# A conditioned transformer block on one core: the head's fills and loads in another order, the key path first, the queries all ended in block 0, first scores among the last maxima, two places of maxima ahead of the loop instead of three

## The chip, the cores and the metric

The kernel runs on one core of a Trainium2 chip. The metric is the device time of one execution in microseconds (us), as the median of several. A core has TensorE (PE; its weight loads are listed as PEld), VectorE (DVE), ScalarE (ACT) and GpSimd (POOL), and queues through which SyncE (SP) and ScalarE start transfers (DMA) between memory and the on-chip buffers. Each engine works through its own instructions strictly in their order, and waits at an instruction until the semaphores that it names have been raised. TensorE writes into eight banks of accumulators, from which VectorE and ScalarE read; a bank is free again when it has been read.

## What is computed

```python
mod = (_silu(c) @ w_mod).reshape(c.shape[0], 6, 1, -1)
sa, ca, ga, sb, cb, gb = (mod[:, 0], mod[:, 1], mod[:, 2], mod[:, 3], mod[:, 4], mod[:, 5])
h = _layernorm(x, axis=-1) * (1 + ca) + sa
x = x + ga * _A_ref(h, A_wq, A_wk, A_wv, A_wo)
h = _layernorm(x, axis=-1) * (1 + cb) + sb
x = x + gb * _B_ref(h, B_w1, B_w2)
```

x has 2048 rows of 512. `_A_ref` is attention with 32 query heads of 16 over one shared key head and one shared value head, softmax over all 2048 keys, then the output projection. `_B_ref` is a dense layer to 1792, relu, and a dense layer back to 512. All is float32.

## The kernel before

**Units and rounds.** The queries are cut into 8 blocks of 256 rows and 4 groups of 8 heads: 32 units. The main loop (L949) has 256 rounds, eight to a unit, two key tiles to a round. In a round stand 8 scores (`scores`, L802: a product into a `ps_exp` bank, exp on ScalarE into a `pe` tile), 8 products with the values (`values`, L936, into `ps_pv`) of scores made before, 8 maxima (`max_of`, L465: a product into a `ps_max`, `ps_more` or `ps_fill` bank, reduced by VectorE, L476) of the unit that comes next, and one portion of dense work (L171): query projections in block 0, and from block 1 on the output projection and the dense layers of the block before. Two strings, `PARTS` and `SHORT` (L43, without a portion), set the order of these within the two halves of a round. A "place" of maxima is eight of them, both halves of the heads over four key blocks of 512 columns; a unit has eight places.

**The maxima's way back.** A score is exp(q k - max), with the maximum put into the product itself: two rows of the query tile `qp` hold the negated maximum, as a high and a low part. When a unit's last maximum has been reduced (L478), VectorE transposes them (`sq<-negm`, L439), ScalarE and GpSimd split them into `ms`, and SP stores them to memory (`mdr<-ms`, L446, four transfers of 16 partitions each) and loads them back in another layout (`qp<-mdr`, L452, two transfers). Stores are issued in the next round's first half; the load stands at that round's end (L963). The unit's first score stands in the second half of the last round of the unit before it.

**The head.** Ahead of the loop stand the modulation vectors, the row norms of x, its transposition to `hT`, keys and values (`kv`, L334: four products over the depth, then evictions, then transposes of the values: five steps for each of four blocks of 512 rows), the first `HEAD_Q` = 5 of 16 query units, and 64 + `LEAD` = 88 maxima: all 64 of unit 0 and three places of unit 1. The queries go to memory (`qdr<-qq`, L370, three transfers each) and come back as `qp` tiles (`load_q`, L417). Loads of x, of the weights and of the modulation matrix `wmod` are issued by SP in program order; eight transfers are in flight at a time. The order of the head's steps is the string `FIRST` (L36), read one letter at a time (L888): `A`, `B` the two halves of the first query unit; `q` two products of a query unit (four letters to a unit); `k` a step of `kv`; `t` four transposes and their eviction; `x`, `y` row statistics on VectorE, `s` on ScalarE; `c`, `e`/`E`, `r`, `f`, `g` the scale of rows and its application; `o` half of a modulation row; `w` a product that only keeps TensorE busy; `m` one maximum; `L`, `l` loads of `qp` for units 0 and 1, and at `L` also of the four later modulation matrices. After the last letter four first scores of the loop are made (L926).

The start, ahead of the string: 32 products of the identity (`warm(32)`, L861), the condition `c` loaded as a column (L78), its silu, two modulation rows (L192) turned into columns, the first block's rows normalized on ScalarE and GpSimd (L307) and transposed with the modulation applied in the eviction (`tr1`, L318). GpSimd copies the keys' and values' weights to their layout (L137) and then fills `kp` and `vt` (L138, L139).

The query units 5 to 13 are the dense portions of block 0 (27 rounds of 32); units 14 and 15 stand in block 1, in its first three rounds and among the seven rounds in which it waits for the second row norm (L573 to L576).

## Time and profile before

| | |
|---|---|
| median of 3 runs | 1631.83 us (1631.66 to 1633.18) |
| the profiled execution | 1633.18 us |
| its span, first to last instruction | 1631.2 us |
| first value products of the loop | 99.9 us into the span |
| from 467 to 1560 us: TensorE, VectorE, ScalarE busy | 1092.5, 926.8, 868.7 of 1093 us |
| last stretch, 1560 to 1631.2: TensorE, VectorE busy | 65.0, 19.9 of 71.2 us |
| granted TensorE clock, mean over the span | 0.996 |

Times in the trace are counted from the span's start; the two microseconds between span and time lie outside it. Matmuls are pipelined and their ends are modelled, so TensorE reads as busy also where it is held for a bank; what holds it is seen in the idle time of the weight loads and in the chain of waits, which follows the work that ended last back to what released it. Each float32 product of the dense steps appears as two records.

### The profile page before, as it was taken

To read this page: it belongs to the slowest core of one execution; us is meant where nothing else is said; L and a number is where in the kernel's file an instruction comes from. 1 tells how busy PE (TensorE), PEld (TensorE's weight loads), DVE (VectorE), ACT (ScalarE), POOL (GpSimd) and SP (SyncE) were. 2 spreads that over 40 slices of the span, in tenths; PEclk is the share of its full clock that TensorE was granted. 3 is DMA by queue.
4 is the path that set the end of the run, shared out by engine and by line. 5 is a ranking of instruction groups with operands and counts; after the bars stand their busy time and mean duration, and the time that the engine had idled before them with its cause. 6 is when DMAs were issued, how large, how long until landed. Compare 5 with 4: busy or idle time off the path is not lost.

```text
span 1631.2 us, 33611 instructions
## 1 busy us (share of the span) xinstructions
PE 1612.9 (99%) x12948; PEld 909.7 (56%) x12948; DVE 1348.6 (83%) x2341; ACT 1212.6 (74%) x2372; POOL 386.5 (24%) x588
## 2 busy tenths in 40 slices
PE   8999999999999999999999999999999999999999
PEld 6545553546654565546654565546654565546668
DVE  5888889898889888998889888898889888997031
ACT  4557778778877887778877887778877887778831
POOL 3313466241113111141113111141113111141110
PEclk9999999999999999999999999999999999999999
DMA  8225633214211331213211331213211231113331
GB/s 280 87 73 170 210 95 106 80 44 125 82 30 46 91 103 33 62 42 114 81 30 48 89 102 34 61 43 113 81 30 49 88 99 37 61 43 104 123 114 57
DMA packets 96718, 137.16 MB, mean 84 GB/s; under 512 B 24564, under 2 KB 60084, under 8 KB 96560
## 3 DMA queue, kind: packets, MB, share of 16 engines
q1 hardware_dynamic: 94848, 134.89, 27.4%
q8 instruction: 103, 1.69, 0.4%
q14 instruction: 55, 0.45, 0.1%
q10 hardware_dynamic: 1712, 0.13, 0.1%
HBM read 104.00 MB, written 28.82 MB: 81 GB/s over the span
## 4 chain that ended last, share of the span: by engine, by line
PE 92%; DVE 3%; ACT 3%; DMA 2%; issue 0%; SPq 0%; POOL 0%; POOLq 0%; ACTq 0%; DVEq 0%
PE ps_pv L943 31%; PE ps_exp L806 21%; PE ps_fill L171 19%; PE ps_max L474 17%; DVE pm L476 2%; ACT pe L808 2%; PE ps_exp L154 1%; PE ps_max L154 1%; PE ps_exp L339 1%; PE ps_fill L154 1%; DMA xb<-in_A_x_dram 1%; DMA wq<-in_A_wq_dram 1%; ACT pvs L818 0%; PE ps_exp L325 0%; DMA qp<-qdr 0%
## 5 line engine op out<-in xcount | busy, mean ns | idle before, releaser
L476 DVE TENSOR_REDUCE pm<-ps_max 128x1 f32<-128x512 f32 x2006 | 1245.7, 682 | 157.6 <-PE ps_max L474 114.7
L808 ACT ACTIVATE pe<-ps_exp 128x512 f32<-128x512 f32 x2048 | 1079.5, 605 | 301.1 <-PE ps_exp L806 143.2
L474 PE MATMUL ps_max<-kp,qp 48*128 48x512 f32 x2006 | 829.6, 425 | 3.1 <-DMA qp<-qdr 2.6
L806 PE MATMUL ps_exp<-qp,kp 50*128 50x512 f32 x2048 | 764.6, 416 | 5.4 <-ACT pe L808 4.4
L943 PE MATMUL ps_pv<-pe,vt 128*32 128x512 f32 x4096 | 546.8, 605 | 0.0
L806 PEld LDWEIGHTS ps_exp<-qp,kp 50*128 50x128 f32 x2048 | 360.0, 186 | 277.9 <-ACT pe L808 187.0
L474 PEld LDWEIGHTS ps_max<-kp,qp 48*128 48x128 f32 x2006 | 366.4, 185 | 248.1 <-DVE pm L476 214.4
L171 PE MATMUL ps_fill<-w2r,r 64*128 64x512 f32 x1044 | 285.7, 404 | 0.0
L171 PE MATMUL ps_fill<-hh,w1s 64*128 64x256 f32 x1568 | 227.8, 285 | 0.0
L171 PEld LDWEIGHTS ps_fill<-hh,w1s 64*128 64x128 f32 x1568 | 204.3, 185 | 6.9 <-PEq L164 6.7
L171 PEld LDWEIGHTS ps_fill<-w2r,r 64*128 64x128 f32 x1044 | 181.9, 184 | 11.2 <-PEq L164 2.5
L943 PEld LDWEIGHTS ps_pv<-pe,vt 128*32 128x32 f32 x4096 | 81.0, 108 | 125.9 <-issue 106.3
L253 POOL TENSOR_TENSOR r<-stg,r 128x512 fp32r<-128x512 f32 x49 | 62.8, 1282 | 321.3 <-ACT r L252 314.4
L171 PE MATMUL ps_fill<-hl,w1s 64*128 64x256 f32 x784 | 126.8, 281 | 0.0
L171 PEld LDWEIGHTS ps_fill<-hl,w1s 64*128 64x128 f32 x784 | 104.7, 185 | 0.0
L171 PE MATMUL ps_fill<-hT,wq 64*128 64x256 f32 x352 | 100.8, 404 | 0.0
L985 POOL TENSOR_TENSOR on<-num,den 128x256 f32<-128x256 f32 x31 | 22.8, 735 | 220.6 <-DMA den<-recs 165.7
L171 PEld LDWEIGHTS ps_fill<-hT,wq 64*128 64x128 f32 x352 | 60.4, 189 | 3.1 <-DVE pm L476 0.4
L822 POOL COPY num<-pvs 128x256 f32<-128x256 f32 x32 | 12.7, 396 | 177.7 <-ACT pvs L818 177.7
L264 ACT ACTIVATE stg<-ps_fill 128x512 f32<-128x512 f32 x64 | 39.4, 616 | 4.9 <-PE ps_fill L154 4.9
L277 POOL TENSOR_TENSOR x<-stg,x 128x512 f32<-128x512 f32 x14 | 18.1, 1291 | 97.8 <-ACT stg L276 97.8
L253 POOL TENSOR_TENSOR ms<-sq,ms 128x32 fp32r<-128x32 f32 x32 | 8.2, 255 | 131.2 <-ACT ms L252 131.2
(158 smaller groups left out, 965.2 us busy)
## 6 DMA issues: line engine op xcount, KB each, us to landing
w1s<-w1dr SPq DMA_DIRECT2D x104, 512.0 KB
qp<-qdr SPq DMA_DIRECT2D x64, 192.0 KB
qdr<-qq SPq DMA_DIRECT2D x45, 256.0 KB
raw<-in_B_w_dram SPq DMA_DIRECT2D x28, 256.0 KB
w1dr<-w1s SPq DMA_DIRECT2D x14, 512.0 KB
wmod<-in_w_mod_dram SPq DMA_DIRECT2D x6, 1024.0 KB
x<-in_A_x_dram SPq DMA_DIRECT2D x8, 512.0 KB
out_dram<-ot SPq DMA_DIRECT2D x16, 256.0 KB
```

The lines of the kernel that those rows point to most:

```text
L154: nc.tensor.matmul(pt, w, a, start=start, stop=stop)
L171: ins = nc.tensor.matmul(pt, w[r], a[r], start=start and h == 1, stop=stop and h == 0)
L253: (eng or nc.gpsimd).tensor_tensor(lo, src, hi.bitcast(F32), op=OP.subtract)
L264: nc.scalar.activation(stg, pt, func, **kw)
L277: nc.gpsimd.tensor_tensor(dst, stg, other, op=OP.add)
L339: nc.tensor.matmul(pt, wkv[:, k * P:(k + 1) * P], hT[b][:, k], start=k == 0, stop=k == DC - 1)
L474: nc.tensor.matmul(pt, qps[u][i][r, j * P:(j + 1) * P], kp[r, kb * 512:(kb + 1) * 512], start=True, stop=True)
L476: nc.vector.tensor_reduce(pms[u][:, (hf * 2 + i) * 4 + j, kb:kb + 1], pt, axis=AX.X, op=OP.max)
L806: nc.tensor.matmul(pt, kp[r, kt * P:(kt + 1) * P], qps[u][ct // 2][r], start=True, stop=True)
L808: nc.scalar.activation(pe, pt, AF.Exp)
L943: nc.tensor.matmul(pvt[at:at + 32], vt[:, kt], pes.pop((s, i)), start=(kt == 0), stop=(kt == KT - 1))
L985: due[1]()
```

## The change

The start: `c` is loaded as four rows and transposed by TensorE (a `ps_max` bank), with the 32 warm-ups spread over four places. `wk` and `wv` are loaded by SP, behind the first query weight, and copied by GpSimd after the first rows' normalization; the fills of `kp`, `vt` and `firsts` go first. x of the fourth block and two query weights are loaded only at letter `L`, behind the queries' way back. The first block's transposes are issued two blocks of depth ahead of the second modulation column (`tr_first`), the last of the four in the `ps_fill` bank.

The string: `L` stands behind the first half of the first query unit; the first block's keys come ahead of its second half; 80 maxima, 20 query steps (six units in the head) and eight letters `d`, each one first score of the loop, among the last maxima. Round 0 has no first-half scores left.

The loop: query units 6 to 15 are all portions of block 0, and block 1's places for them are empty. The negated maxima are stored in two transfers of 128 partitions instead of four of 16, and loaded in the second half of the same round.

```diff
-LEAD = 24
-HEAD_Q = 5
-FIRST = ("AkxqxsycyqkyBkkytqELqttmmmkmmsqkrktsmmmmkkmsmommmmttqftm"
-         "mmmogtkmmmkkmmmmkktmmlmmtqmmqtmmmmkkktmmmmkkmmmmqwmmmqmk"
-         "mmmommmqmmmqmmmommmqmmqmmommmommmqmmmommqmmmommmmmmm")
+LEAD = 16
+HEAD_Q = 6
+FIRST = ("AxkkLkxxxkcwqyqkyyywBEmmmmqttqtktkmmsrmmkkmsmmmqttmmmmqs"
+         "sqtmmmmkkkfmmmmqktmmmmqgkqmmmmttqqtmmmmkkkmmmmtkmmkmmmom"
+         "mmqommmmqkmmommmqmmlmqmmmommqommmmqqqmmomddmmdmmdodmmmdd"
+         "mdo")
...
-    ccol = cst.tile([P, DC], F32, name="ccol")
-    nc.scalar.dma_start(ccol, c[0].rearrange("(k p) -> p k", p=P), allow_slow_non_contiguous=True)
+    crow = cst.tile([DC, P], F32, name="crow")
+    nc.scalar.dma_start(crow, c[0].rearrange("(k p) -> k p", p=P))
...
-    wkv0 = sb.tile([P, DC, 2, DH], F32, name="wkv0", tag="tmp", bufs=2)
-    nc.scalar.dma_start(wkv0[:, :, 0], chunks(wk))
-    nc.scalar.dma_start(wkv0[:, :, 1], chunks(wv))
...
     load_wq(0)
-    for b in range(1, NL):
-        load_x(b)
-        load_wq(b)
+    wkv0 = sb.tile([P, DC, 2, DH], F32, name="wkv0", tag="stg", bufs=3)
+    nc.sync.dma_start(wkv0[:, :, 0], chunks(wk))
+    nc.sync.dma_start(wkv0[:, :, 1], chunks(wv))
+    load_x(1)
+    load_wq(1)
+    load_x(2)
...
-    for j in range(8):
-        nc.gpsimd.tensor_copy(wkvr[:, :, j], wkv0[:, :, 1 if j % 4 == 3 else 0])
-    nc.gpsimd.memset(kp.bitcast(F32), 1.0)
-    nc.gpsimd.memset(vt, 1.0)
...
+    warm(4)
+    ccol = ps_max()[:, 0:DC]
+    nc.tensor.transpose(ccol, crow, idn[0:DC, 0:DC])
+    warm(22)
...
+    def tr_first():
+
+        h = hT[0] = sb.tile([P, DC, LB], F32, name="hT", tag="big", bufs=4)
+        pts = [turn_rows(0, k) for k in range(2)]
+        yield
+        for k in range(DC):
+            if k == 0:
+                pts += [turn_rows(0, 2), turn_rows(0, 3, ps_fill)]
+            if k % 2:
+                nc.vector.tensor_scalar(h[:, k], pts[k], cols[:, 1, k:k + 1], cols[:, 0, k:k + 1],
+                                        op0=OP.mult, op1=OP.add)
...
-            for q in range(4):
-                nc.sync.dma_start(mdr[:, :, q].rearrange("p a n -> a p n"),
-                                  ms[q * 32:q * 32 + 16].bitcast(F32))
+            for e in range(2):
+                nc.sync.dma_start(mdr[e].rearrange("a q n -> q a n"), ms[:, e].bitcast(F32))
...
-            qqs = [sb.tile([P, 2, LB], F32R, name="qq", tag="w1s", bufs=3) for _ in range(2)]
-            rest, fill = [others_of(14 + n, qqs[n]) for n in range(2)]
-            fill = itertools.chain([[]] * 3, fill, [[]])
+            rest, fill = iter([[]] * 3), [[]] * 7
...
-        for n in range(HEAD_Q, 14):
+        for n in range(HEAD_Q, 16):
...
     run(sums_of(0))
     row1 = mod_row(1, ps_max())
     ln1_rows(0, *ln1_ends(mvs[0], True))
+    warm(4)
+    for j in range(8):
+        nc.gpsimd.tensor_copy(wkvr[:, :, j], wkv0[:, :, 1 if j % 4 == 3 else 0])
+    mod_col(row1, 1, True, ps_max())
+    warm(2)
     row0 = mod_row(0, ps_max())
-    mod_col(row1, 1, True, ps_max())
+    first_rows = tr_first()
+    next(first_rows)
+    mod_col(row0, 0, False, ps_max())
+    run(first_rows)
...
+    early = [(s, ct) for cts in ((1, 3), (0, 2)) for s in range(2) for ct in cts]
...
             load_q(0)
+            load_x(3)
+            for n in (2, 3):
+                load_wq(n)
             for i in (2, 5, 3, 4):
                 load_mod(i)
...
+        elif what == "d":
+            scores(*early.pop(0))
...
-    for s, ct in ((0, 1), (0, 3), (1, 1), (1, 3)):
-        scores(s, ct)
...
-            c=[partial(scores, *n) for n in ((s, 0), (s, 2), (s + 1, 0), (s + 1, 2))],
+            c=[partial(scores, *n) for n in ((s, 0), (s, 2), (s + 1, 0), (s + 1, 2)) if c],
...
-            ends.append((c, load))
+            half_later.append(load)
```

How the rows move is shown at three places. First SP's queue in the head, from the loads of x to the first queries' way back (`xb` are blocks of x, `wq` query weights, `qdr` the queries in memory, `qp` the query tiles, `wmod` modulation); before:

```order
L97 DMA xb<-in_A_x_dram 128x512 x4
L111 DMA wq_82<-in_A_wq_dram 128x4x128
L99 DMA xb<-in_A_x_dram 128x4x512
L111 DMA wq_83<-in_A_wq_dram 128x4x128
L99 DMA xb<-in_A_x_dram 128x4x512
L111 DMA wq_83<-in_A_wq_dram 128x4x128
L370 DMA qdr_0_123<-qq 8x16x256 x6
L423 DMA qp<-qdr_0_123 48x4x256 x2
L90 DMA wmod<-in_w_mod_dram 128x4x512 x4
```

and with the change:

```order
L113 DMA wkv_82<-in_A_wk_dram 128x4x16
L114 DMA wkv_82<-in_A_wv_dram 128x4x16
L98 DMA xb<-in_A_x_dram 128x512 x4
L106 DMA wq_70<-in_A_wq_dram 128x4x128
L100 DMA xb<-in_A_x_dram 128x4x512
L388 DMA qdr_0_119<-qq 8x16x256 x3
L441 DMA qp<-qdr_0_119 48x4x256 x2
L100 DMA xb<-in_A_x_dram 128x4x512
L106 DMA wq_71<-in_A_wq_dram 128x4x128 x2
L91 DMA wmod<-in_w_mod_dram 128x4x512 x4
```

The first read of `qp` stands behind three stores instead of six, and the fourth block of x and two weights have moved behind it.

Second, TensorE where the head passes into round 0 (`ps_max`, `ps_more`: maxima; `ps_exp<-qp,kp`: scores; `ps_fill<-hT`: query projections, the first product with the values follows); before:

```order
L474 MATMUL ps_max<-kp,qp 128x512 x3
L474 MATMUL ps_more<-kp,qp 128x512
L806 MATMUL ps_exp<-qp,kp 128x512 x5
L474 MATMUL ps_max<-kp,qp 128x512
L806 MATMUL ps_exp<-qp,kp 128x512
L474 MATMUL ps_max<-kp,qp 128x512
L171 MATMUL ps_fill<-hT,wq_82 128x256
```

and with the change:

```order
L823 MATMUL ps_exp<-qp,kp 128x512
L195 MATMUL ps_exp<-wmod,sgb 32x512 x4
L823 MATMUL ps_exp<-qp,kp 128x512
L491 MATMUL ps_max<-kp,qp 128x512 x3
L823 MATMUL ps_exp<-qp,kp 128x512 x2
L491 MATMUL ps_more<-kp,qp 128x512
L823 MATMUL ps_exp<-qp,kp 128x512
L205 MATMUL ps_exp<-mrow,firsts 128x512
L491 MATMUL ps_max<-kp,qp 128x512 x2
L174 MATMUL ps_fill<-hT,wq_71 128x256
```

The scores have moved up among the last maxima and modulation rows, and round 0 begins with maxima and a query projection.

Third, SP's queue at one unit's negated maxima in the loop, in a block with dense layers (`w1s` are the first layer's weights, `recs` and `den` the softmax sums of the unit before); before:

```order
L844 DMA den<-recs 128x1x256
L501 DMA w1s<-w1dr_115 128x1024
L423 DMA qp<-qdr_0_135 48x4x256 x2
L501 DMA w1s<-w1dr_116 128x1024
L501 DMA w1s<-w1dr_117 128x1024
L446 DMA mdr<-ms 16x2x32 x4
L501 DMA w1s<-w1dr_118 128x1024
L452 DMA qp<-mdr 2x1024 x2
```

and with the change:

```order
L861 DMA den<-recs 128x1x256
L518 DMA w1s<-w1dr_111 128x1024
L518 DMA w1s<-w1dr_112 128x1024
L441 DMA qp<-qdr_0_131 48x4x256 x2
L518 DMA w1s<-w1dr_113 128x1024
L518 DMA w1s<-w1dr_114 128x1024
L464 DMA mdr<-ms 4x32x32 x2
L469 DMA qp<-mdr 2x1024 x2
```

The stores are two, the load stands right behind them, and the weight load that stood between has moved to after it.

More of the change, by code (lines that the diff above doesn't have):

```diff
@@ L99, in load_x @@
             nc.sync.dma_start(xb1[b], chunks(x[b * LB:(b + 1) * LB]))
-    wkv0 = sb.tile([P, DC, 2, DH], F32, name="wkv0", tag="tmp", bufs=2)
-    nc.scalar.dma_start(wkv0[:, :, 0], chunks(wk))
-    nc.scalar.dma_start(wkv0[:, :, 1], chunks(wv))
-    load_x(0)
-    load_mod(1)
-    load_mod(0)
     wq2 = [sb.tile([P, 2, DC, P], F32, name="wq2", tag="x1", bufs=2) for _ in range(2)]
@@ L111, in load_wq @@
         nc.sync.dma_start(wqf[j], chunks(wq[:, j * P:(j + 1) * P]))
+    load_x(0)
+    load_mod(1)
+    load_mod(0)
     load_wq(0)
-    for b in range(1, NL):
-        load_x(b)
-        load_wq(b)
+    wkv0 = sb.tile([P, DC, 2, DH], F32, name="wkv0", tag="stg", bufs=3)
[4 more added lines that the diff above has]
+    load_x(2)
     idn = cst.tile([P, P], F32, name="idn")
@@ L130, in build @@
     qdr = [[dr.tile([8, 48, LB], F32R, name=f"qdr{b}_{j}") for j in range(NG)] for b in range(NL)]
+    nc.gpsimd.memset(kp.bitcast(F32), 1.0)
+    nc.gpsimd.memset(vt, 1.0)
+    firsts = cst.tile([P, P], F32, name="firsts")
+    nc.gpsimd.memset(firsts, 0.0)
+    for k in range(DC):
+        nc.gpsimd.memset(firsts[k * 32:k * 32 + 1], 1.0)
     wkv = sb.tile([P, 512], F32, name="wkv", tag="pvs", bufs=1)
     wkvr = wkv.rearrange("p (k a n) -> p k a n", k=DC, a=8)
-    for j in range(8):
-        nc.gpsimd.tensor_copy(wkvr[:, :, j], wkv0[:, :, 1 if j % 4 == 3 else 0])
-    nc.gpsimd.memset(kp.bitcast(F32), 1.0)
-    nc.gpsimd.memset(vt, 1.0)
     def warm(n):
@@ L183, in build @@
     nc.vector.tensor_copy(sgb, sg[:, :, None].to_broadcast(sgb.shape))
-    firsts = cst.tile([P, P], F32, name="firsts")
-    nc.gpsimd.memset(firsts, 0.0)
-    for k in range(DC):
-        nc.gpsimd.memset(firsts[k * 32:k * 32 + 1], 1.0)
     def mod_row(i, pt):
@@ L316, in ln1_rows, with turn_rows @@
                                      bias=nmy[:, n], scale=y[:, n])
+    def turn_rows(b, k, bank=ps_exp):
+        pt = bank()
+        for t in range(4):
+            nc.tensor.transpose(pt[:, t * P:(t + 1) * P], xb1[b][:, t, k * P:(k + 1) * P], idn)
+        return pt
     def tr1(b):
-        xb = xb1[b]
         h = hT[b] = sb.tile([P, DC, LB], F32, name="hT", tag="big", bufs=4)
         for k in range(DC):
-            pt = ps_exp()
-            for t in range(4):
-                nc.tensor.transpose(pt[:, t * P:(t + 1) * P], xb[:, t, k * P:(k + 1) * P], idn)
-            if b == 0 and k % 2:
-                nc.vector.tensor_scalar(h[:, k], pt, cols[:, 1, k:k + 1], cols[:, 0, k:k + 1],
+            pt = turn_rows(b, k)
+            nc.scalar.activation(h[:, k], pt, AF.Identity,
+                                 bias=cols[:, 0, k:k + 1], scale=cols[:, 1, k:k + 1])
+            yield
+    def tr_first():
+        h = hT[0] = sb.tile([P, DC, LB], F32, name="hT", tag="big", bufs=4)
+        pts = [turn_rows(0, k) for k in range(2)]
+        yield
+        for k in range(DC):
+            if k == 0:
+                pts += [turn_rows(0, 2), turn_rows(0, 3, ps_fill)]
+            if k % 2:
+                nc.vector.tensor_scalar(h[:, k], pts[k], cols[:, 1, k:k + 1], cols[:, 0, k:k + 1],
                                         op0=OP.mult, op1=OP.add)
             else:
-                nc.scalar.activation(h[:, k], pt, AF.Identity,
+                nc.scalar.activation(h[:, k], pts[k], AF.Identity,
                                      bias=cols[:, 0, k:k + 1], scale=cols[:, 1, k:k + 1])
-            yield
+        yield
     def kv(b):
@@ L383, in first_queries, with qproj @@
             yield
-    def qproj(b, j, bank, qq=None):
+    def qproj(b, j, bank):
         pt = bank()
@@ L396, in end @@
         def end():
-            qt = qq if qq is not None else sb.tile([P, 2, LB], F32R, name="qq", tag="t4", bufs=2)
+            qt = sb.tile([P, 2, LB], F32R, name="qq", tag="t4", bufs=2)
             stg = sb.tile([P, 512], F32, name="stg", tag="tmp", bufs=2)
@@ L439, in max_rows @@
         nc.vector.transpose(sq, negm)
-        mdr = dr.tile([2, 16, 4, 32], F32, name="mdr", tag="mdr", bufs=4)
+        mdr = dr.tile([2, 32, 4, 32], F32, name="mdr", tag="mdr", bufs=4)
         def parts():
@@ L481, in max_of @@
             later.append(max_rows(u, negm))
-    banks = [ps_max, ps_max, ps_max, ps_more] * 22
+    banks = [ps_max, ps_max, ps_max, ps_more] * ((64 + LEAD) // 4)
     places = [(0, i, j) for i in range(2) for j in range(4)]
@@ L744, in build, with others_of @@
     gr = sb.tile([P, 2, D], F32, name="gr", tag="xn", bufs=1)
-    def others_of(n, qq=None):
-        todo, end = qproj(*divmod(n, NG), ps_fill, qq=qq)
+    def others_of(n):
+        todo, end = qproj(*divmod(n, NG), ps_fill)
         for i in range(0, len(todo), 3):
@@ L799, in chores @@
             yield
+    pes = {}
     def scores(s, ct):
@@ L856, in build @@
     todo = chores()
-    trs = [tr1(b) for b in range(NL)]
+    trs = [tr1(b) for b in range(1, NL)]
     kvs = [kv(b) for b in range(NL)]
-    warm(32)
     mvs = [ln_mv(4) for _ in range(NL)]
@@ L871, in build @@
     ln1_rows(0, *ln1_ends(mvs[0], True))
+    warm(4)
[3 more added lines that the diff above has]
+    warm(2)
     row0 = mod_row(0, ps_max())
-    mod_col(row1, 1, True, ps_max())
+    first_rows = tr_first()
+    next(first_rows)
+    mod_col(row0, 0, False, ps_max())
+    run(first_rows)
     sums1, sums2, sums3 = sums_of(1), sums_of(2), iter(range(4))
-    next(sums1)
-    mod_col(row0, 0, False, ps_max())
-    next(sums1)
-    run(trs[0])
     queries0 = first_queries()
@@ L884, in build @@
                                      for n in range(1, HEAD_Q))),
-                 t=itertools.chain(*trs[1:]), k=itertools.chain(*kvs),
+                 t=itertools.chain(*trs), k=itertools.chain(*kvs),
                  o=itertools.chain(*mods))
+    early = [(s, ct) for cts in ((1, 3), (0, 2)) for s in range(2) for ct in cts]
     waiting, ready = list(first_max), 0
@@ L918, in build @@
         put_off.clear()
-    assert not waiting
+    assert not waiting and not early
     for step in steps.values():
         assert next(step, "end") == "end"
-    pes = {}
-    for s, ct in ((0, 1), (0, 3), (1, 1), (1, 3)):
-        scores(s, ct)
     others = queries()
```

## The prediction, as put on record

> **What bounds the kernel now.** I read the page first, then a table of busy time by stage, then VectorE's timeline and the chain of waits for the head (everything ahead of the loop of 256 rounds).

> ```profile
> PE 1612.9 (99%) x12948; PEld 909.7 (56%) x12948; DVE 1348.6 (83%) x2341; ACT 1212.6 (74%) x2372; POOL 386.5 (24%) x588
> 30.00:42.00 12.00, 9.13 (x31) 5.00 (x31) 6.00 (x13) 5.90 (x12) 5.55 (x17) 0.72 0.97 334
> 42.00:68.00 26.00, 26.00 (x121) 13.62 (x121) 22.63 (x41) 17.05 (x31) 10.40 (x20) 1.00 0.32 109
> 68.00:97.00 29.00, 28.46 (x119) 13.68 (x119) 28.93 (x51) 9.06 (x17) 5.32 (x5) 0.97 0.19 53
> 467.00:1560.00 1093.00, 1092.47 (x9336) 608.92 (x9336) 926.84 (x1589) 868.66 (x1709) 216.38 (x352) 1.00 0.24 69
> ```

> The last four rows are stretches: length, then busy time of PE, PEld, DVE, ACT and POOL with counts, then granted clock, DMA share and GB/s. The loop is TensorE's: 1092.47 of 1093.00. The head has three parts. From 30 to 42 nothing is full and the clock falls to 0.72; from 42 to 68 TensorE is full; from 68 to 97 VectorE is (28.93 of 29.00), while TensorE has little left. Work of the two engines that could overlap is done one after the other.

> ```profile
> 20.05 9.97 SPq L370 DMA_DIRECT2D qdr<-qq  x6
> 34.43 0.69 DVE L476 TENSOR_REDUCE pm<-ps_max 128x1 f32<-128x512 f32 x1 [1.47 <-PE ps_max L474]
> 42.40 1.29 DVE L476 TENSOR_REDUCE pm<-ps_max 128x1 f32<-128x512 f32 x2 [4.48 <-PE ps_max L474]
> 96.46 0.68 DVE L476 TENSOR_REDUCE pm<-ps_more 128x1 f32<-128x512 f32 x1
> ```

> These are the store of the first queries, the first maximum, the sixth and seventh, and the 88th and last. Now the chain of waits:

> ```profile
> 30.19 3.49 DMA qp<-qdr
> 72.73 9.57 DVE pm L476 x16
> 99.93 1.86 PE ps_pv L943 x8
> 106.83 1.00 PE ps_pv L943 x8
> ```

> The queries are read back only behind the sixth store, at 30.19, and are there at 33.7; then five maxima, then 4.48 us of nothing. One maximum is 9.57/16 = 0.60 us. The first value products of rounds 0 and 1 start at 99.9 and 106.8.

> **Start.** Warm-ups, the modulation load, a GpSimd memset and the first query product:

> ```profile
> 1.34 9.96 PE L145 MATMUL ps_exp<-idn 128*128 128x128 f32 x64 [1.34 <-POOL idn masks.py:199]
> 8.19 1.80 POOL L138 MEMSET kp<- 128x2048 f32 x1
> 8.53 2.10 DVE L228 TENSOR_SCALAR ve<-mv 128x4 f32<-128x4 f32 x1
> 12.59 1.06 PE L192 MATMUL ps_max<-wmod,sgb 128*32 128x512 f32 x8 [0.29 <-DMA wmod<-in_w_mod_dram]
> 17.62 1.98 PE L378 MATMUL ps_exp<-hT,wq 128*128 128x256 f32 x8
> ```

> A 128x4 operation held VectorE for 2.10 us while GpSimd filled kp; that memset now runs in the first microseconds, so the row statistics end 2 us earlier. But this is not all gained. The 32 warm-ups stay (0.31 us each), ten of them now between the modulation rows, and the second row still wants its load, there at 12.59. Walking it: 22 warm-ups end at 9.9, row 1.0, four warm-ups 1.25, four transposes 0.5, two warm-ups 0.6, second row 13.3 to 14.3, eight transposes 1.0, the column 0.7, two pairs of evictions of 0.8, and the first query product ends at about 18.6 instead of 17.62 + 1.98 = 19.6. **Minus 1.0** (bounds 0 and -2.1, the whole of the stall). The condition row by a contiguous load and a transpose arrives before the weights do, so it costs nothing; the keys' weights, now in SP's queue, land behind 3.25 MB of x and modulation, at some 14.5, and are copied by 16, ahead of their first use at 18.6.

> **The rest of the head.** The read of the first queries now stands behind three stores instead of six, and x of the fourth block and two weights stand behind it. Stores at 19 to 20.5, landing at 22, read for the same 3.5: there at 25.6. From the start of the first query product (16.8) TensorE has two half queries (3.6), five key steps (4.2), two query steps (1.9) and two warm-ups (0.6) to do ahead of the first maximum, 10.3 by the prices below; so it asks at 27.1 and does not wait. So the head becomes TensorE's, and its length is a sum of prices:

> ```profile
> 54.91 1.91 PE ps_exp L339 x4
> 58.52 0.87 PE ps_fill L154 x4
> 59.81 1.06 PE ps_fill L154 x4
> 48.71 0.44 PE ps_exp L325 x4
> 61.31 0.66 PE ps_max L474 x3
> 110.66 0.65 PE ps_exp L806 x2
> ```

> A key step is 1.91/2 = 0.955 (16 of them, and 4 x 0.36 for the values' transposes: 16.7). A query step is 0.97, the mean of 0.87 and 1.06: 20 steps, 19.4 (16 before). A step of transposes is 0.44 and a gap, 0.5: 12, 6.0. A modulation step is 1.0 (row at 12.59): 8, 8.0. Four maxima, of which the row names three, take 0.66: 80, 13.6 with gaps. A score is 0.33: 8, 2.6. The two half queries 1.8 each, two warm-ups 0.6. Sum 70.5; from 16.8 on, 87.3. VectorE's 80 maxima are 80 x 0.60 = 48 of that, so it is no longer the longer of the two. The same prices on the old order between 42 and 67 give 25.2 for 25.3 measured, so a full TensorE keeps to them.

> I add 2 us for small stalls (rows of the third block from GpSimd, statistics on ScalarE in front of an eviction, the first score behind the negated maxima): head ends at 89.3. Bounds: 0, and 6, which is the 1.47 + 4.48 that VectorE lost before. Round 0 now has its first-half scores done, so four maxima pace it (2.4): first values at 91.7, round 1 at 97.5 instead of 106.8. **Minus 9.3** in all, the start's 1.0 included (bounds -11.3 and -5.3). The eight maxima taken out pay no price on TensorE worth naming; what pays is that the maxima run under TensorE's work.

> **The loop.** Value products of one round to those of a later one:

> ```profile
> 126.99 1.00 PE ps_pv L943 x8
> 132.77 1.00 PE ps_pv L943 x8
> 259.74 1.00 PE ps_pv L943 x8
> 265.01 0.99 PE ps_pv L943 x8
> 343.16 1.00 PE ps_pv L943 x8
> 361.12 1.00 PE ps_pv L943 x8
> 1499.52 0.99 PE ps_pv L943 x8
> 1505.22 0.99 PE ps_pv L943 x8
> 1510.68 0.99 PE ps_pv L943 x8
> ```

> A round with a third of a query unit takes 5.78, one with no dense work 5.27. Block 0 now carries ten units, not nine: three rounds more at +0.51, **plus 1.5**. Block 1 loses two units. One unit stood in its first three rounds, -1.5; the other between 343.16 and 361.12, three rounds in 17.96 where idle ones take 15.8, -2.1: **minus 3.6** (bounds -2.5 and -4.5, for how the rounds beside them settle). The last place of maxima moves from the head to a round that had none, 5.46 against 5.70: **plus 0.25**.

> **The negated maxima.** With one place fewer ahead of the loop, each unit's last maximum falls one round later, while its first score stays. What has to fit in between, for one unit of block 2 and, in the last three rows, one of block 0:

> ```profile
> L439 DVE STREAM_TRANSPOSE sq<-negm x1: 213/213/213, 586.5 to 586.5; 128x32 f32<-128x32 f32 x1
> 589.68 1.72 SPq L446 DMA_DIRECT2D mdr<-ms  x4
> 592.59 0.54 SPq L452 DMA_DIRECT2D qp<-mdr  x2
> 600.52 0.40 PE L806 MATMUL ps_exp<-qp,kp 50*128 50x512 f32 x1
> 220.97 0.21 DVE L439 STREAM_TRANSPOSE sq<-negm 128x32 f32<-128x32 f32 x1
> 224.62 3.48 SPq L446 DMA_DIRECT2D mdr<-ms  x4
> 230.47 0.54 SPq L452 DMA_DIRECT2D qp<-mdr  x2
> ```

> From the transpose to the first score are 14.0 us now, 8.3 after. In block 2 four stores end 4.9 after it, the load starts 1.2 later. Two stores instead of four end 0.86 earlier, so the load is issued by +5.8. Its landing no row shows; taken like the store's (1.2) it is there at +7.0, with the slower gap below (2.4) at +8.2. Both fit in 8.3: nothing for the 27 units from block 1 on. In block 0 the query's own stores stand ahead in the same queue and the memory is busy: the load starts 9.5 after the transpose. Less two stores that is some 8 to 8.6, landing at 10 to 11 where 8.3 is at hand: 2 us late, in those units whose last maximum meets the end of a query unit (every third round), units 1 and 4. I take **plus 2.4** for block 0 (bounds 0 and 6). What waits behind the late score is all of TensorE.

> [...]

> Sum: -9.3 + 1.5 - 3.6 + 0.25 + 2.4 = -8.75. The profiled execution took 1633.18 (span 1631.2 and 2.0 around it) and would take 1624.4; the median of the runs, 1631.83, lies 1.35 under it, so the forecast is **1623.0**.

> **Rivals.** *No stall at all* (0.15). The 2.0 of the head and the 2.4 of block 0 fall away: 1623.0 - 4.4 = 1618.6. For it: the full stretch 42 to 68 kept its prices without a gap. Against: 224.62, a store held for 3.48.

> *The head stalls again* (0.12). The second block's rows come late, as before 42.40, and TensorE, idle, runs at 0.72 of its clock: 6 us of the gain are gone, 1629. For it: statistics of two blocks, the keys' low halves and the row scale stand in one VectorE row ahead of the first maximum, so this one comes only 3 us sooner than 34.43. Against: x of the fourth block no longer blocks ScalarE there. [...]

> *Every boundary is late* (0.11): slower. If the stores' gap is 2.4 everywhere and the load's too, and the load is issued after the dense weights in SP's queue at +7.0, it lands at +9.4, 1.1 late in 27 units: +30 on top of the -8.75, 1653. It decides from 0.4 us per unit on. For it: 1.3 us or less of room per unit. Against: the block 2 rows, with four stores.

> **Numbers.** The forecast, from 1619.5 to 1627, has 0.62. The range 1616.5 to 1629 takes in the first rival and most of the second; the third is left out. 0.2% (3.3 us) is about what a measurement tells from no change. Faster by more: 0.62 + 0.15 + 0.04 of the second rival, 0.81; within: 0.07; slower: 0.11 and a hundredth of the second, 0.12.

> **What would show it.** First query product ended near 18.6; clock 1.00 through 26 to 42; first maximum near 31.5 and no idle of VectorE over 1 us ahead of the sixth; values of round 1 at 96 to 99; rounds 32 to 34 and 42 to 45 at 5.3; scores of units 1 and 4 waiting on the load of the negated maxima, those of later units not. Wrong if round 1 starts after 101, or if TensorE waits for that load in blocks 1 to 7.

## The result and the profile after

The changed kernel takes 1641.65 us (median of 10, 1634.97 to 1643.17); the kernel before, beside it, 1632.9 (1631.66 to 1633.6). The ratio, taken from all runs and not from the two medians, is 1.0046, 95% interval 1.0032 to 1.0059: slower by half a percent, where faster was forecast. Seven of the ten executions took 1639.7 to 1643.2 at a mean granted clock of 0.991 or 0.992, three took 1635.0 to 1636.4 at 0.995 or 0.996. The profiled one is of the seven: 1643.17, span 1641.3.

The page's line of busy time; TensorE is at 99%, as before:

```profile
PE 1619.0 (99%) x12935; PEld 911.3 (56%) x12935; DVE 1347.2 (82%) x2341; ACT 1213.0 (74%) x2372; POOL 387.8 (24%) x588
```

The four stretches that the prediction showed of before (length; busy PE, PEld, DVE, ACT, POOL; granted clock; DMA share; GB/s):

```profile
30.00:42.00 12.00, 11.90 (x56) 7.26 (x55) 11.11 (x24) 10.86 (x23) 8.04 (x19) 1.00 1.05 374
42.00:68.00 26.00, 26.00 (x122) 14.55 (x122) 21.67 (x40) 15.83 (x30) 11.82 (x22) 1.00 0.45 144
68.00:97.00 29.00, 27.44 (x107) 13.78 (x108) 20.65 (x36) 11.37 (x20) 4.67 (x5) 0.81 0.31 84
467.00:1560.00 1093.00, 1092.43 (x9348) 609.66 (x9344) 940.57 (x1610) 867.67 (x1707) 216.85 (x353) 1.00 0.23 69
```

The first two rows are what was forecast: TensorE is full from 30 to 68 and keeps its clock (0.72 before). The third is not: the clock is 0.81 from 68 to 97. The long stretch is the loop's, as before.

From the starts of the rounds' value products the whole difference can be told by sections:

| | before | changed | difference | forecast |
|---|---|---|---|---|
| start of round 1 | 106.77 | 106.71 | -0.1 | -9.3 |
| rounds 1 to 32 (block 0) | 176.71 | 189.17 | +12.5 | +1.5 and +2.4 |
| rounds 32 to 64 (block 1) | 183.80 | 180.86 | -2.9 | -3.6 |
| round 64 to the end | 1163.97 | 1164.59 | +0.6 | +0.25 |
| span | 1631.2 | 1641.3 | +10.1 | -8.75 |

The chain of waits of the changed kernel around the head's end (start, length, what):

```profile
78.45 0.22 DVE sq L457
...
79.73 4.56 DMA mdr<-ms
...
84.65 1.48 DMA qp<-mdr
86.17 0.79 PE ps_exp L823
...
89.10 1.86 PE ps_exp L195 x8
...
99.10 1.86 PE ps_pv L966 x8
...
106.78 0.99 PE ps_pv L966 x8
```

TensorE's weight loads at that place (idle time ahead of a row, and what ended it, in brackets):

```profile
84.12 0.18 PEld L491 LDWEIGHTS ps_more<-kp,qp 48*128 48x128 f32 x1 [0.76 <-DVE pm L493]
86.17 0.28 PEld L823 LDWEIGHTS ps_exp<-qp,kp 50*128 50x128 f32 x1 [1.87 <-DMA qp<-mdr]
```

This is the way of unit 0's negated maxima: transposed at 78.45, stored, landed 4.56 us later, loaded, and at 86.17 there for the first score, the first `d` of the string, for which TensorE's weight loads sat idle 1.87 us. What comes after it takes nearly double: a modulation row 1.86 where it took 1.06 before, eight value products 1.86 where they take 0.99.

The same in block 0. VectorE's transposition of unit 1's maxima (its times of start):

```profile
L457 DVE STREAM_TRANSPOSE sq<-negm x1: 211/211/211, 134.1 to 134.1; 128x32 f32<-128x32 f32 x1
```

What SP issues behind it:

```profile
135.80 1.94 SPq L388 DMA_DIRECT2D qdr<-qq  x3
137.85 3.15 SPq L464 DMA_DIRECT2D mdr<-ms  x2
143.72 0.57 SPq L469 DMA_DIRECT2D qp<-mdr  x2
```

Pieces of the chain of waits for unit 1, and for unit 4:

```profile
139.22 4.44 DMA mdr<-ms
...
144.03 1.63 DMA qp<-mdr
145.70 0.50 PE ps_exp L823
...
282.97 4.63 DMA mdr<-ms
```

The idle time of the scores' weight loads that ended with this load, over the whole span (us, times):

```profile
  DMA qp<-mdr: 10.1, 3
```

Three stores of a query unit go first in SP's queue; the load is issued 9.6 us after the transposition, and the score starts at 11.6. Three scores in all wait for such a load, 10.1 us together: those of units 0 (1.87), 1 (3.14) and 4 (5.08). The first scores of units 1 and 4 stand in rounds 7 and 31. Round 7 takes 10.54 instead of 5.78 and round 31 11.55 instead of 5.39, 10.9 us of block 0's 12.5; and round 32 takes 6.08, where 5.26 is a round with no dense work.

Last, TensorE's clock, in stretches cut where it switches:

```profile
82.72:86.14 3.42, 1.89 (x5) 0.58 (x5) 1.98 (x3) 1.82 (x3) 1.26 (x1) 1.00 0.09 21
86.14:103.20 17.06, 17.03 (x56) 8.60 (x57) 8.77 (x14) 6.55 (x12) 1.88 (x2) 0.50 0.36 92
140.75:144.16 3.41, 2.12 (x15) 0.64 (x13) 2.43 (x4) 1.28 (x3) 0.00 (x0) 1.00 0.32 94
144.16:147.58 3.42, 1.88 (x17) 1.51 (x21) 1.01 (x2) 1.35 (x3) 0.00 (x0) 1.00 0.71 222
147.58:150.99 3.41, 3.41 (x17) 1.46 (x17) 1.56 (x3) 2.10 (x5) 0.84 (x2) 0.50 0.04 13
284.11:287.52 3.41, 1.32 (x10) 0.20 (x8) 1.65 (x3) 1.20 (x3) 0.21 (x1) 1.00 0.37 111
287.52:297.76 10.24, 8.15 (x34) 2.65 (x34) 4.97 (x8) 4.75 (x9) 3.21 (x4) 0.50 0.11 34
```

The three waits left TensorE busy 1.89, 1.88 and 1.32 us of the first, fourth and sixth stretch; behind each the clock is 0.50, for 17.06, 3.41 and 10.24 us. So each of these three waits is paid twice: its length, and then the stretch at 0.50.

### The profile page after: what moved, and what is told of

It reads as the page before. It is cut to its first block, busy times and chain, and to the rows that moved or that the text cites. A ratio compares the mean times of both kernels' runs of the same rounds, so it can differ in the third digit from the quotient of the medians.

```text
span 1641.3 us, 33525 instructions
## 1 busy us (share of the span) xinstructions
PE 1619.0 (99%) x12935; PEld 911.3 (56%) x12935; DVE 1347.2 (82%) x2341; ACT 1213.0 (74%) x2372; POOL 387.8 (24%) x588
## 4 chain that ended last, share of the span: by engine, by line
PE 92%; ACT 3%; DVE 2%; DMA 1%; issue 0%; POOL 0%; POOLq 0%; SPq 0%; ACTq 0%; DVEq 0%
PE ps_pv L966 30%; PE ps_exp L823 21%; PE ps_fill L174 18%; PE ps_max L491 17%; ACT pe L825 2%; DVE pm L493 1%; PE ps_exp L157 1%; PE ps_max L157 1%; PE ps_fill L157 1%; DMA mdr<-ms 1%; PE ps_exp L357 1%; PE ps_exp L148 1%; PE ps_exp L324 0%; ACT stg L279 0%; DMA qp<-mdr 0%
## 5 line engine op out<-in xcount | busy, mean ns | idle before, releaser
L174 PEld LDWEIGHTS ps_fill<-w2r,r 64*128 64x128 f32 x1044 | 182.0, 185 | 11.3 <-PEq L167 2.5
L174 PE MATMUL ps_fill<-hT,wq 64*128 64x256 f32 x320 | 92.9, 408 | 0.0
L174 PEld LDWEIGHTS ps_fill<-hT,wq 64*128 64x128 f32 x320 | 56.2, 192 | 3.1
L256 POOL TENSOR_TENSOR hl<-xh,hh 128x512 fp32r<-128x512 f32 x14 | 17.7, 1286 | 119.5 <-ACT hh L255 119.5
```

What stands on the lines that cost most here:

```text
L174: ins = nc.tensor.matmul(pt, w[r], a[r], start=start and h == 1, stop=stop and h == 0)
L256: (eng or nc.gpsimd).tensor_tensor(lo, src, hi.bitcast(F32), op=OP.subtract)
```

## The experiments

Two theories, which do not exclude each other, and a rival to each. In the head: the idle time ahead of the first score halves the clock (rival: the first scores are slow for another reason). In block 0: the negated maxima are late because their transfers and their split stand behind a query unit's in the same queues (rival: two transfers of 128 partitions are themselves slower than four of 16). All kernels are the changed kernel with one to three edits, each measured beside the kernel before; the ratios are to that kernel. Three dots in a line of a string stand for letters left out.

### Seven products in the idle time

Each `w` is a product of the identity that needs no load.

```diff
-         "...qqqmmomddmmdmmdodmmmdd"
+         "...qqqmmomwwwwwwwddmmdmmdodmmmdd"
```

> Change of this run against the changed kernel (its ten runs: 1641.65 median, 1634.97 to 1643.17): seven products of the identity (2.2 us) stand directly ahead of the first score in the head, where TensorE waited 1.56 us for the negated maxima and its clock then read 0.50 from 90 to 100 us. Theory, idleness: the clock falls because TensorE stands idle there, and the slow products from 86 to 104 us are what the seven slow runs of ten lost. Then the clock stays at 1.0 through 80 to 110, the loop's round 1 starts near 100.5 instead of 106.7, and all runs lie at 1634 to 1636. Rival, density: the clock falls because the head now keeps TensorE full for 70 us (or for another reason outside the wait). Then it falls again, round 1 starts at 106 to 107, and the median stays at 1641 to 1642.

1634.28 us (11 runs, 1632.84 to 1636.57); ratio 1.0012, interval 1.0004 to 1.0021. Two stretches of the profile, the one that was ahead of the drop in the changed kernel's, and one that lay in it:

```profile
82.72:86.14 3.42, 3.40 (x22) 2.40 (x21) 1.51 (x3) 1.02 (x3) 1.27 (x1) 1.00 0.16 20
90.00:100.00 10.00, 10.00 (x66) 5.03 (x68) 8.87 (x15) 5.63 (x11) 1.90 (x2) 1.00 0.31 86
```

The transposition of unit 0's maxima, and TensorE's weight loads:

```profile
77.53 0.21 DVE L457 STREAM_TRANSPOSE sq<-negm 128x32 f32<-128x32 f32 x1
83.20 0.18 PEld L491 LDWEIGHTS ps_more<-kp,qp 48*128 48x128 f32 x1 [0.76 <-DVE pm L493]
83.62 1.74 PEld L148 LDWEIGHTS ps_exp<-idn 128*128 128x128 f32 x14 [0.24 <-issue]
85.55 0.18 PEld L823 LDWEIGHTS ps_exp<-qp,kp 50*128 50x128 f32 x1 [0.19 <-PE ps_exp L148]
```

The first score starts no earlier after the maximum ahead of it than without the products (2.35 us after 83.20; 2.05 after 84.12 in the changed kernel). It now follows the products, and its load is as late as it was: issued at 83.50, 6.0 us after the transposition, for 5.9 in the changed kernel. But here the clock stays 1.00, and round 1 starts at 98.73 instead of 106.71. Of these 8.0 us, 0.9 were there already at the transposition (77.53 for 78.45), ahead of the edit; from there on it is 7.1, and by the medians 7.4. So in the head the 2 us of waiting cost little, and the half clock behind them 7 to 8. Rounds 7 and 31 are about as long as in the changed kernel (10.65 and 11.04).

### The stores first in the queue

`put_off` holds, in order, what is issued in the next round's first half: the split and the stores of a query unit and of the negated maxima. `half_later` holds the load, issued in that round's second half.

```diff
-            put_off.append(parts)
+            put_off.insert(0, parts)
```

> Against the changed kernel: in the loop the split and the stores of the negated maxima are put ahead of those of a query unit that ended in the same round; nothing else. Theory, queue order: units 1 and 4 come late (10.5 and 11.6 us for their round instead of 5.8 and 5.4) because GpSimd and SP handle the query unit's 786 KB first. Then their stores start 1.2 us after the transpose as in the other units instead of 3.7, the load is issued by +6, the two rounds fall to 5.8 and 5.3, and the median drops by 10 to 12, to about 1631. Rival, memory: the stores of 128-byte rows land late because the memory is busy in block 0, whatever stands ahead in the queue. Then the load still starts 8 us or more after the transpose and the median drops by less than 4.

> Both edits together. If idleness and queue order both hold, the two are in different places and add: 1641.65 - 6.5 - 11 = 1624 (the forecast on record was 1623.0), tight within 1 us, clock 0.998 or more. If only the queue order holds: 1630 to 1631. If only idleness holds: 1634 to 1636.

1637.53 us (12 runs, 1629.26 to 1639.78; ratio 1.0020, 1.0006 to 1.0034), and with the seven products 1631.72 (11 runs; 0.9991, 0.9983 to 1.0000): better by 4.1 and 2.6, and short of what was expected. SP's issues for unit 1, whose maxima are transposed at 131.9, without the products:

```profile
133.22 1.19 SPq L464 DMA_DIRECT2D mdr<-ms  x2
134.51 1.92 SPq L388 DMA_DIRECT2D qdr<-qq  x3
136.53 0.89 SPq L469 DMA_DIRECT2D qp<-mdr  x2
```

The piece of the chain behind them:

```profile
137.17 5.27 DMA qp<-mdr
```

The stores now start 1.3 us after the transposition instead of 3.7, since the split of the maxima no longer stands behind the query's on ScalarE and GpSimd, and are issued in 1.19 us. But the query's three stores slip between them and the load, and the load lands 5.27 us after its issue instead of 1.63. The lateness moved from the store to the load: what is behind 768 KB (the three stores; 786 thousand bytes) in the queue waits, whichever it is.

### Stores and load first

```diff
-            put_off.append(parts)
-            half_later.append(load)
+            put_off[:0] = [parts, load]
```

> Against the changed kernel (1641.65; rounds 7 and 31 take 10.5 and 11.6 us) and against the run with the maxima's stores first (1637.53; rounds 11.1 and 9.7, the load issued 5 us after the transpose but only usable 10 us after it): now the load of the negated maxima stands ahead of the query unit's stores in SP's queue as well. Theory, one queue: what is issued first is moved first; in the run before, 786 KB of query stores and a 512 KB weight store stood ahead of the load in the transfer engines. Then the load lands by +6 to +7, rounds 7 and 31 fall to 5.8 and 5.3, and the median drops by 11 to 1630 or 1631. Rival, memory: small transfers are slow whenever the memory is busy. Then the rounds stay above 8 us and the median at 1637 or more.

1628.74 us (10 runs); ratio 0.9974, 0.9961 to 0.9986. SP's issues for unit 1:

```profile
133.14 1.18 SPq L464 DMA_DIRECT2D mdr<-ms  x2
135.77 0.56 SPq L469 DMA_DIRECT2D qp<-mdr  x2
```

Two stretches of the head:

```profile
83.22:86.64 3.42, 1.77 (x9) 1.04 (x9) 1.29 (x3) 1.25 (x3) 1.26 (x1) 1.00 0.21 34
86.64:100.29 13.65, 13.65 (x45) 6.11 (x45) 7.49 (x13) 4.90 (x9) 1.89 (x2) 0.50 0.38 108
```

The load is issued 1.45 us after the stores' end, ahead of the query's stores. Rounds 7, 31 and 32 take 5.77, 5.36 and 5.26, so block 0 has no wait left: the theory of the one queue holds. The edit does not touch the head, and the drop there came in some executions only: three took 1622.8 to 1623.4 at a mean clock of 1.000, seven 1628.6 to 1631.1 at 0.995 or 0.996.

### The form of the stores

```diff
-        mdr = dr.tile([2, 32, 4, 32], F32, name="mdr", tag="mdr", bufs=4)
+        mdr = dr.tile([2, 16, 4, 32], F32, name="mdr", tag="mdr", bufs=4)
...
-            for e in range(2):
-                nc.sync.dma_start(mdr[e].rearrange("a q n -> q a n"), ms[:, e].bitcast(F32))
+            for q in range(4):
+                nc.sync.dma_start(mdr[:, :, q].rearrange("p a n -> a p n"),
+                                  ms[q * 32:q * 32 + 16].bitcast(F32))
```

> Against the changed kernel: the negated maxima go to memory in four stores of 16 partitions, as before the change; nothing else. Theory, one queue: the form is not what is late, so round 1, 7 and 31 keep their times within 1 us (the four issues take 0.9 us longer): 1641 to 1643. Rival: the store of 128 rows is what is late: the first score comes 2 to 3 us sooner, the clock stays up, units 1 and 4 gain 2 us each, and the median is below 1636.

1645.73 us (4 runs, 1642.87 to 1646.61); ratio 1.0086, 1.0070 to 1.0101. For unit 1:

```profile
129.04 3.84 SPq L464 DMA_DIRECT2D mdr<-ms  x4
136.03 0.54 SPq L470 DMA_DIRECT2D qp<-mdr  x2
```

Four stores are issued in 3.84 us where two take 3.15, and the load follows the first issue by 6.99 instead of 5.87. In unit 1 two transfers are 1 us better; in unit 4 they gain nothing, since the load is issued 9.60 us after the transposition with four and 9.65 with two. Units 1 and 4 are as late as in the changed kernel or later (rounds 7 and 31 take 11.66 and 11.33), and the median did not fall below 1636: the rival falls. The median is 3 us above what was expected. The head missed the expectation the other way: in the profiled execution, the fastest of the four, the first score waited 1.55 instead of 1.87 us, the clock stayed 1.00 there, and round 1 started at 97.89. The last section comes back to this.

### The fifth query unit behind unit 0's last maximum

```diff
-         "...mmlmqmmmommqomm..."
+         "...mmlmmmmommqoqmm..."
```

> Against the changed kernel: in the head's string the last step of the fifth query unit stands behind the last maximum of unit 0, so that its three stores (786 KB) follow the stores of the negated maxima instead of preceding them. Theory, one queue: the stores of the negated maxima took 4.56 us to land because they stood behind those; now they land in about 1.5 us, as in the loop, the first score does not wait, the clock stays at 1.0, round 1 starts at 98 instead of 106.7, and the median is 1632 to 1634, with no fill. Rival: the two-part store itself is slow (256 rows of 128 bytes): the first score waits still, the clock falls, 1640 to 1642.

1637.26 us (7 runs, 1633.29 to 1638.86); ratio 1.0025, 1.0014 to 1.0036. The store lands 1.5 us after its issue ends, as expected, since no query store is ahead of it any more, and the first score's wait is gone. The median missed the expected 1632 to 1634: in the profiled run the clock was lost at another place (0.83 from 70 to 80, where VectorE was busy for 9.42 of 10 us; 1.00 from 80 to 120), and block 0 kept its waits (rounds 7 and 31 take 9.11 and 11.40).

### The lead of eight maxima

```diff
-LEAD = 16
+LEAD = 24
-         "mdo")
+         "mdommmmmmmm")
```

The second kernel puts the eight ahead of the first score instead; the third has them last and the seven products too.

> Against the changed kernel: three places of maxima ahead of the loop again instead of two (eight more maxima as the last letters of the head). Theory, lateness: with a round more of slack (14.3 us instead of 8.6) units 1 and 4 are on time; -11 in block 0, -0.25 at the end, and + 3 to 5 for eight maxima in the head (VectorE's 0.60 each, some of it while TensorE's clock is low): 1634 to 1636. Rival: the rounds of units 1 and 4 are long for a reason other than the late load (the query portions that now run to round 29, the empty rounds after it). Then rounds 7 and 31 stay at 10 us and more, and the median is 1644 or above.

> Against the run with three places of maxima whose eight additional ones stood last (1629.87, clock 0.50 from 90 to 100): the eight stand directly ahead of the first score, where they fill TensorE's wait as the seven idle products did. Theory: the clock stays at 1.0, the eight maxima cost VectorE's 4.8 us less the 2 us of the wait, round 1 starts at 101 to 103 instead of 107.9, and the median is 1623 to 1626, faster than both kernels. Rival: eight maxima held by VectorE (TensorE computes 0.16 of each 0.60 us) are too thin to keep the clock up: it falls as before, 1629 to 1631.

> Three places of maxima ahead of the loop as before the change (the eight more as the last letters) and seven products ahead of the first score. Theory (the lead of eight maxima removes the wait in block 0, the products the one in the head): the head's gain over the lead alone, 1629.9, is 4 to 6 us: 1624 to 1626, round 1 at 101 to 102 at full clock, since the eight maxima are VectorE's (8 x 0.60 less what TensorE has beside them), rounds 7 and 31 at 5.8 and 5.4. Rival (the eight maxima at the end leave TensorE thin, and the clock falls after all): 1628 or more, 0.50 or so in 90 to 110.

1629.87 (12 runs; ratio 0.9993, 0.9983 to 1.0002), 1630.94 (11 runs; 0.9989, 0.9980 to 0.9998) and 1630.01 (11 runs; 0.9990, 0.9981 to 0.9998). With the third place of maxima back, rounds 7 and 31 take 5.8 and 5.4 in all three: each unit has a round more for its way back, and the lateness costs nothing. The first kernel came 4 us under what was expected; the second and third came out as their rivals said. For the head gains little. In the first kernel the first score still waits for its load, 1.90 us, and the clock halves for 17.07; in the other two no score waits for the load, and the clock halves all the same. Two stretches of the second kernel:

```profile
86.20:89.62 3.42, 2.91 (x10) 1.05 (x9) 3.42 (x7) 1.14 (x3) 0.00 (x0) 1.00 0.52 140
89.62:106.68 17.06, 17.06 (x57) 7.88 (x61) 10.45 (x17) 6.74 (x12) 1.88 (x2) 0.50 0.34 89
```

And two of the third:

```profile
90.91:94.32 3.41, 2.77 (x9) 1.18 (x8) 3.26 (x6) 0.60 (x1) 0.00 (x0) 1.00 0.91 218
94.32:101.15 6.83, 6.72 (x25) 3.17 (x26) 4.73 (x9) 0.00 (x0) 1.88 (x2) 0.50 0.13 37
```

VectorE is (nearly) full in the first row of each pair (3.42, 3.26) and TensorE only follows it, ten and nine products in a window. Then its clock halves, with or without the seven products. So maxima that VectorE paces may fail to keep the clock up. They do not always: in the head of the changed kernel, from 34.00 to 37.40, VectorE is full (3.40 of 3.40), TensorE has ten products, modelled as busy for 3.30, and the clock stays 1.00 there and up to 86.14. What decides between such windows was not tested.

### Both causes removed

> Seven products ahead of the first score, and the store and the load of the negated maxima first in SP's queue. Theory (two separate causes: the idle of 2 us in the head that halves the clock, and the one queue in block 0): the gains add. From the kernel with the seven products alone, 1634.3, go the 10.5 us that its rounds 7, 31 and 32 were too long (10.65 and 11.04 where 5.77 and 5.36 stand without a wait): 1623 to 1624.5, all runs within 2 us, round 1 at 98.7, rounds 7 and 31 at 5.8 and 5.4, clock 0.998 or more. Rival (they share a cause: without the one, the other costs less): 1626 to 1629, and a round of block 0 over 6.5.

> As before, but three products ahead of the first score instead of seven, so that about half of the idle time stays (some 1 us). Theory (the length of an idle stretch decides over the clock, and 1 us is short enough): 1623 to 1624.5, clock 1.00 through 80 to 110. Rival (any such gap can halve the clock): some of the runs near 1629, as with the load first and no product at all, and 0.50 in one of the three stretches when the profiled run is one of them.

> No products; the fifth query unit ends after the last maximum, so that its stores stand behind those of the negated maxima, and the load goes first in block 0 as well. Theory (two causes that add, and a shorter wait for the first score loses little): the 1637.3 of the one alone less the 9 to 10.5 us of rounds 7, 31 and 32: 1626 to 1628. Rival (this order's head keeps the clock by luck): runs spread over 5 us or more, median 1629 or above.

1623.48 us (5 runs, 1623.32 to 1623.83; ratio 0.9952, 0.9940 to 0.9964), 1623.18 (6 runs, five of them 1622.48 to 1623.34, one 1629.55; 0.9957, 0.9942 to 0.9971) and 1622.69 (5 runs, 1621.90 to 1624.71; 0.9949, 0.9937 to 0.9961). All three are faster than both kernels, by some 0.5% and 1.1%. The chain's value products of rounds 1, 32 and 64 in the first of the three:

```profile
99.33 0.97 PE ps_pv L966 x5
...
277.32 1.04 PE ps_pv L966 x8
...
457.34 1.00 PE ps_pv L966 x8
```

SP's issues in the head of the third:

```profile
78.95 1.17 SPq L464 DMA_DIRECT2D mdr<-ms  x2
81.56 0.55 SPq L469 DMA_DIRECT2D qp<-mdr  x2
```

And its first score's weight load, with no wait ahead of it:

```profile
85.46 0.18 PEld L823 LDWEIGHTS ps_exp<-qp,kp 50*128 50x128 f32 x1
```

The two causes nearly add: 7.4 for the products alone and 12.9 for the load alone, 20.3 together, against 18.2 measured with both. With the load first the products are worth 5.3 and not 7.4; in the profile of that kernel the half clock in the head lasted 13.65 us where the changed kernel had 17.06; 3.41 us less at half speed are worth up to 1.7, most of the difference. In the third kernel nothing fills the time; the load is issued at 81.56 instead of 84.34, the first score does not wait, and the granted clock is 1.00 over the span in the profile. It came 3 us under its expectation, which had been reckoned from the median of an order (1637.26) whose profiled head had a drop of the clock in it. With three products 0.7 us of TensorE's wait are left in the profile. The one run at 1629.55 had a mean clock of 0.996; it was not profiled, and where it lost its clock is open. It is what the rival expected (some runs near 1629), so it is not shown that so short a wait is always harmless.

## Why the prediction was wrong

By its own steps:

- **Start, -1.0.** The first query product ended at 19.1 instead of 18.6: a gain of 0.5. The step's own walk, which has the product start at 16.8, gives 18.8.
- **The head's sum.** The order did nearly what was said: clock 1.00 from 26 to 42, no idle of VectorE over 1 us ahead of the sixth maximum, the first at 32.9 (31.5 forecast). With both causes removed round 1 starts at 99.26, 7.5 earlier than before, for the 9.3 forecast: 1.8 too long, inside the bounds.
- **"I add 2 us for small stalls (..., the first score behind the negated maxima)".** This step failed. The stall was named and its length was right (1.87 us of idle weight loads). What was left out is what came behind the wait: 17 us at half clock, 7 to 8 us lost with the products left out against with them in (8.0 by the starts of round 1, 7.1 from the transposition on, 7.4 by the medians), most of the gain. The rival *The head stalls again* had the clock in its price (1629), but for another stall, the second block's rows, which did not come. The lengths at 0.50 in the changed kernel are 3.41, 10.24 and 17.06 us, the last two three and five times the first. Why the one in the head lasted so long, with TensorE modelled as busy throughout (17.03 of 17.06), is open.
- **Block 0, three more query rounds, +1.5.** With the causes removed rounds 1 to 32 take 178.0 for 176.7: +1.3. Right.
- **"Less two stores that is some 8 to 8.6, landing at 10 to 11 ... plus 2.4".** This step failed too. The place was right (units 1 and 4, no other of the loop), the size was not. The load was issued 9.6 after the transposition, where before, with four stores, it was 9.5, and the score came at 11.6 in both units, where 8.3 was at hand. The 0.86 us was taken from block 2, where the stores find the queue empty; here they stand behind 768 KB of queries, and what counts is when these are through. The scores' weight loads sat idle 3.14 and 5.08 us, and the clock halved both times: 11.7 in all, with round 32. Besides, 2 us in each of two units are 4 by the step's own words, and 2.4 was taken.
- **Block 1, -3.6.** -2.9 in the changed kernel, whose round 32 began at half clock and took 0.8 longer; -3.8 with the causes removed (180.01). Right.
- **The last place of maxima, +0.25.** +0.6, and +0.3 (1164.26) with the causes removed. Right.
- ***Every boundary is late*** did not happen: of the 32 first scores three waited for the load. Its landing, which no row had shown, took 1.48 us after the issue in the head and 1.63 in unit 1 (1.2 was taken).

Without these waits and their clock the sections sum to -7.5 + 1.3 - 3.8 + 0.3 = -9.7, span 1621.5. That the kernels without them come out at the forecast 1623.0 is in part luck: the head is 1.8 longer than forecast, and the 2.4 of block 0 is gone. Work and prices were read rightly to within the bounds given; what failed is the price of three waits, one of 2 us in the head and two of 3 and 5 us in block 0, and of the half clock behind each.

## What to carry to other kernels

A wait of TensorE is priced as its length plus the half clock that may follow it: here a wait of 1.9 us cost 7 to 8. Either give the wait enough lead, or put products that need nothing into it. And a small transfer that something waits for is placed by what stands ahead of it in its queue, store and load alike: count the bytes there, not the number of its own transfers. Here the load landed 5.27 us after its issue behind three query stores of 786 thousand bytes, and 1.63 without them, and behind a query unit's stores it was issued 9.5 us after the transposition with four stores of the maxima (before) and 9.6 with two.

## What the runs showed of the hardware

Cut from these ends into pieces of 3.41 us, six that stand right ahead of a stretch at 0.50 have TensorE busy for little: 0.79 us of 3.41 (before, 30.62 to 34.03), 1.89, 1.88 and 1.32 (changed, above), 1.77 (stores and load first, above) and 1.94 (three places, the eight last, 83.41 to 86.82). Three have it busy for more: 3.08 (before, below), 2.91 and 2.77 (three places, above), all three with VectorE full or nearly so. In the head and the loop of the kernel before and of the changed one no other piece at full clock has TensorE busy for under 2 us; the next is 140.75 to 144.16 above, which has 2.12 and was not followed by 0.50, while the one behind it (1.88) was. At the end of the changed kernel a piece with 1.83 (1635.79 to 1639.20) was not followed by 0.50 either. The same wait in the head of the kernel with four stores, two pieces side by side, their edges reckoned by the author:

```profile
80.31:83.72 3.41, 3.17 (x11) 1.43 (x9) 2.25 (x5) 1.82 (x3) 0.78 (x1) 1.00 0.21 69
83.72:87.14 3.42, 2.42 (x16) 1.19 (x16) 1.91 (x4) 1.89 (x4) 0.48 (x1) 1.00 0.38 95
```

Cut there, the idle time is 0.24 and 1.00, and the clock stayed 1.00 in the head of that run, where 1.53 in one piece (82.72 to 86.14 of the changed kernel) was followed by 17 us at 0.50. (The idle time is also a little shorter in all, 1.24 for 1.53, so the place of the edge is not shown to be what counts.) Two kernels have two times: some 1635 and 1642 the changed one, and 1623 and 1629 the one with the load first. That the two differ by the clock is seen in the mean clocks of the executions (0.995 or 0.996 against 0.991 or 0.992, and 1.000 against 0.995 or 0.996). That the place of such an edge decides between them was the author's estimate, and is not shown: the shorter executions of those two kernels were not profiled.

The kernel before loses clock there as well: it was 0.50 for 6.83 us at the head's end, behind a piece in which VectorE was full.

```profile
92.06:95.47 3.41, 3.08 (x11) 1.37 (x10) 3.41 (x7) 0.70 (x2) 1.25 (x1) 1.00 0.33 77
95.47:102.30 6.83, 6.72 (x27) 3.11 (x27) 4.43 (x7) 4.15 (x8) 0.00 (x0) 0.50 0.84 214
```
